# Trading the places of six groups in the first channel product of batch 0

## The chip, the cores and the metric

One Trainium2 chip, one core. The metric is the device time of one execution in microseconds. A comparison of this kernel tells about 2% from no change. The profile is of one execution, and its times are counted from the first instruction of the span.

## The reference

Two blocks follow each other. The first is attention over 4 batches, 8 heads, 768 positions and 64 columns a head; a position sees the first 4 positions and a window of 128. The second is an MLP over tokens and channels:

```
x   = attention(q, k, v)               # as 4 x 768 x 512
a1  = alpha1 * x + beta1
u   = x + lam * (w_tok @ a1)           # over the 768 positions
a2  = alpha2 * u + beta2
ch  = max(a2 @ w_ch1, 0) @ w_ch2       # 512 -> 2048 -> 512
out = u + lam * ch
```

The change touches `a2 @ w_ch1` of batch 0 alone.

## The kernel before

All inputs are float32 in HBM; products run in fp16 and gather in PSUM in float32. The program is a list of tasks, each of a few instructions on one engine. No scheduler runs while it is built: `emit` walks the tuple `ORDER` and issues the tasks by number. `ENGINES` gives the engine of each task that has a choice, and `HOMES` the buffer of each tile, so that a tile that needs a buffer waits for the last reader of the tile that had it before. Every engine carries out its tasks in the order in which they were issued.

The first channel product is made by `mlp1` (L921). It is cut into 16 groups of 128 columns of w_ch1 (`fi`, 0 to 15) and two halves of 384 positions (`chk`). A group is four matmuls of 128 x 384 (L929) into one PSUM tile `h`, one for each 128 rows of the depth of 512, followed by a relu that writes `hT`, on ACT (L935) or on DVE (L937). The operand `uT` is a2, transposed; for batch 0 it is made by PE transposes `uTp` (L890) of `u`, which ACT and DVE scale (L873, L875).

The weights w_ch1 are brought in by `load_w1` (L446) in four loads of 512 columns, so a quarter of the columns serves four groups: quarter 0 groups 0 to 3, quarter 1 groups 4 to 7, quarter 2 groups 8 to 11, quarter 3 groups 12 to 15. POOL issues them, one after another, with a conversion to fp16 on the way (L448), into `w1f`, which stays in SBUF for all batches. Each group waits for its quarter. `gate` (L453) puts tiny reads of quarters 1, 2 and 3 into the queue of SP (L455); SP waits at each until that quarter is there, and with it all loads that stand behind in its queue.

Around the place of the change these tasks stand on the engines, in this order. PE: token product `tok` (L849), transposes of the first half, the first groups of the half `chk` 0, then transposes of the second half, more groups, then the groups of `chk` 1, and between them transposes `tp` of batch 1's q and k (L507), its scores `S` (L617) and its products with the values, `pv` (L718). ACT: relus, casts of `u`, casts of q and k of batch 1 (L155). DVE: relus, the scaling of `uT`, and the product of staged w_ch2 with lam (L831, tile `w2f`). POOL: the other half of these products, and casts of the values of batch 1 (L157, tile `vfs`, from the load `vnat`). SP: loads of w_ch2 (L444, staged in four buffers `wst`), of batch 1's q and k (L397) and of its values (L407).

The second channel product of batch 0 (L1114) reads `hT` by quarters in their order and begins after all groups of the first.

Of the kernel before, what the change touches and what calls it, by code (L numbers as in the profile page):

```python
# [77 lines left out]
def kernel(  # L78
# [119 lines left out]
    for r in range(NR):  # L198
# [18 lines left out]
        26, 6, 9, 7, 10, 5, 11, 8, 18, 15, 72, 19, 1, 12, 3, 0, 4, 2, 22, 14, 73, 74, 45, 48, 46,  # L217
        17, 39, 49, 47, 53, 13, 40, 50, 41, 90, 95, 43, 91, 51, 54, 103, 52, 16, 44, 61, 104, 42,
        96, 109, 100, 62, 107, 110, 63, 55, 28, 108, 92, 56, 101, 21, 68, 65, 59, 93, 20, 69, 97,
        102, 111, 94, 24, 98, 57, 60, 30, 112, 105, 23, 58, 99, 113, 128, 106, 114, 116, 25, 131,  # L220
        135, 78, 115, 64, 27, 138, 31, 32, 117, 132, 29, 129, 136, 33, 122, 66, 125, 34, 123, 137,
        119, 139, 126, 35, 79, 70, 120, 140, 124, 84, 71, 80, 133, 130, 141, 67, 146, 85, 134, 121,
        147, 144, 75, 118, 158, 86, 154, 148, 159, 145, 142, 87, 149, 150, 155, 160, 143, 76, 88,
        151, 156, 81, 77, 166, 152, 162, 167, 89, 127, 82, 163, 213, 83, 168, 209, 164, 165, 214,
        210, 153, 217, 179, 211, 178, 157, 197, 229, 36, 212, 215, 218, 185, 216, 226, 230, 219,
        176, 161, 177, 220, 169, 223, 222, 232, 225, 224, 221, 227, 237, 233, 279, 238, 234, 228,
        273, 280, 182, 171, 204, 291, 274, 175, 289, 292, 200, 231, 293, 290, 246, 294, 295, 199,
        384, 241, 248, 188, 186, 257, 296, 247, 172, 243, 277, 174, 181, 242, 259, 258, 187, 170,
        278, 267, 37, 260, 271, 358, 268, 198, 285, 349, 272, 381, 301, 286, 366, 351, 303, 302,
        189, 297, 378, 173, 304, 281, 180, 352, 203, 249, 190, 282, 298, 379, 250, 287, 380, 192,  # L230
        353, 385, 288, 206, 283, 386, 369, 375, 367, 265, 284, 368, 202, 370, 266, 363, 376, 371,
        253, 377, 201, 299, 254, 372, 364, 183, 382, 191, 300, 373, 615, 365, 275, 374, 383, 357,
        261, 276, 408, 262, 387, 263, 184, 409, 205, 195, 239, 411, 264, 410, 395, 269, 396, 240,
        397, 270, 196, 388, 614, 621, 235, 412, 400, 194, 244, 398, 236, 401, 255, 617, 251, 245,
        256, 389, 390, 399, 252, 311, 359, 207, 193, 391, 424, 616, 335, 425, 393, 341, 426, 392,
        336, 648, 427, 634, 413, 394, 312, 636, 414, 428, 419, 404, 420, 415, 360, 405, 313, 429,
        208, 422, 337, 416, 361, 441, 421, 622, 402, 314, 423, 442, 626, 403, 305, 638, 315, 406,
        430, 640, 316, 435, 431, 306, 641, 355, 436, 443, 619, 437, 338, 649, 618, 438, 362, 317,
        432, 637, 407, 307, 433, 345, 444, 339, 439, 635, 318, 445, 450, 434, 639, 644, 319, 451,
        628, 452, 620, 440, 308, 645, 340, 453, 417, 446, 323, 447, 418, 320, 309, 448, 324, 321,  # L240
        658, 322, 329, 449, 642, 659, 454, 325, 625, 643, 330, 646, 347, 455, 326, 623, 343, 647,
        464, 344, 456, 465, 348, 466, 460, 457, 467, 650, 327, 458, 331, 461, 629, 459, 472, 462,
        632, 463, 653, 356, 651, 656, 627, 332, 38, 654, 480, 333, 342, 624, 652, 473, 310, 476,
        468, 471, 470, 469, 481, 474, 488, 885, 477, 475, 482, 492, 655, 490, 493, 350, 483, 478,
        514, 491, 516, 489, 657, 479, 515, 660, 517, 630, 882, 665, 518, 663, 354, 328, 666, 502,
        880, 661, 664, 498, 879, 519, 508, 499, 346, 503, 678, 662, 512, 509, 679, 504, 513, 487,
        484, 671, 485, 676, 486, 506, 677, 877, 548, 505, 672, 680, 507, 526, 549, 546, 527, 631,
        334, 522, 674, 681, 528, 547, 907, 523, 534, 903, 529, 633, 682, 675, 878, 542, 683, 535,
        890, 689, 543, 550, 685, 684, 690, 510, 551, 494, 511, 673, 667, 544, 495, 668, 891, 496,
        686, 545, 901, 687, 669, 497, 693, 888, 688, 883, 530, 694, 670, 700, 531, 524, 897, 701,  # L250
        698, 500, 691, 525, 696, 699, 552, 501, 697, 704, 553, 558, 695, 705, 904, 692, 562, 559,
        706, 909, 887, 707, 563, 564, 898, 708, 702, 566, 565, 910, 715, 703, 567, 532, 716, 889,
        713, 533, 709, 714, 896, 520, 710, 556, 717, 521, 538, 557, 537, 540, 539, 536, 560, 541,
        899, 718, 921, 572, 922, 881, 711, 574, 884, 573, 576, 712, 561, 719, 902, 577, 575, 555,
        727, 720, 569, 908, 721, 580, 728, 578, 722, 581, 729, 554, 723, 905, 730, 568, 739, 724,
        579, 725, 592, 570, 911, 726, 582, 740, 593, 588, 912, 583, 595, 584, 571, 906, 743, 589,
        731, 585, 900, 590, 732, 605, 744, 587, 733, 596, 606, 734, 607, 611, 594, 597, 602, 745,
        612, 586, 613, 599, 895, 603, 591, 757, 765, 600, 758, 601, 759, 766, 741, 771, 760, 742,
        916, 772, 751, 917, 746, 773, 752, 913, 761, 919, 774, 886, 767, 918, 604, 762, 763, 598,
        768, 777, 764, 779, 920, 923, 780, 914, 755, 915, 778, 608, 756, 926, 930, 735, 609, 931,  # L260
        924, 927, 781, 736, 925, 775, 782, 737, 928, 753, 929, 893, 738, 934, 754, 892, 769, 935,
        932, 610, 941, 770, 819, 776, 942, 894, 939, 820, 821, 940, 937, 936, 823, 749, 822, 945,
        748, 824, 938, 747, 827, 933, 948, 950, 750, 952, 943, 951, 825, 953, 787, 828, 944, 807,
        788, 797, 826, 808, 949, 946, 829, 798, 801, 954, 830, 791, 802, 956, 947, 792, 783, 955,
        957, 963, 961, 784, 789, 958, 962, 811, 790, 964, 959, 785, 812, 965, 805, 786, 795, 806,
        960, 967, 796, 799, 793, 968, 966, 970, 972, 794, 813, 971, 969, 815, 973, 814, 809, 800,
        816, 803, 810, 974, 978, 804, 976, 979, 837, 975, 977, 835, 838, 980, 841, 836, 839, 842,
        818, 843, 840, 845, 981, 832, 982, 846, 817, 986, 844, 831, 990, 987, 983, 988, 847, 991,
        984, 851, 833, 992, 1002, 993, 834, 848, 855, 852, 985, 849, 1003, 859, 856, 1004, 989,
        1006, 850, 860, 1005, 853, 998, 1007, 1008, 868, 999, 857, 1009, 997, 865, 995, 858, 862,  # L270
        996, 869, 866, 1000, 874, 994, 854, 1001, 1016, 863, 875, 1040, 1017, 1038, 1041, 1032,
        1039, 871, 1020, 872, 1028, 1021, 1011, 1024, 1029, 1013, 1018, 1033, 1012, 1025, 1034,
        1019, 1036, 1010, 1035, 1042, 1037, 1076, 1043, 1070, 1077, 870, 1074, 1071, 1054, 1075,
        1022, 1055, 1060, 1023, 1048, 1061, 1058, 1049, 1066, 1059, 1014, 1044, 1015, 1067, 1072,
        1045, 1056, 1073, 1026, 1057, 1078, 1068, 1079, 1064, 1069, 1046, 1027, 1050, 1063, 1047,
        1052, 1082, 1053, 1051, 1084, 1083, 1062, 1065, 1030, 1085, 1080, 1101, 1031, 1081, 1091,
        1102, 1107, 1092, 1097, 1093, 1103, 864, 1108, 1105, 867, 1098, 1111, 1106, 1104, 1113,
        1112, 1089, 1114, 1115, 1086, 1116, 1090, 861, 1094, 1087, 1117, 1099, 1109, 1100, 1121,
        1095, 1110, 1125, 1118, 1122, 1124, 1134, 1126, 1123, 1128, 1135, 1127, 1119, 1136, 1088,
        1140, 1120, 873, 876, 1131, 1129, 1141, 1096, 1137, 1142, 1132, 1130, 1133, 1138, 1139,  # L280
    )
    ENGINES = (
        "3313134433443333444444444444444433334441111201201202120212021213030121211201211210200200"
        "2020201202011202020202020213213213213213213202002020202020213121312131213121312131404444"
        "4044413314433334411114413334444042213221321021020121021021321202020020211212021212120212"
        "1212020202120202120212020212020202020212122221022221422221022221422221022221013111111131"
        "1311333333302002002102132002132002102020101212010321213120301212131201012121312010121213"
        "1203212131212131213421342104110121042104213401012020202021202020212120202020212120202121"
# [1034 lines left out]
```

The softmax here doesn't subtract the row's maximum and nothing guards it: scores larger than these inputs give would overflow.

## Time and profile before

| | us |
|---|---|
| runs shown, median (lowest to highest) | 258.79 (256.25 to 259.25), 3 runs |
| span of the profiled execution | 254.3 |
| whole time of the profiled execution | not given beside its span |
| PE busy with matmuls | 245.6 |
| DVE, ACT, POOL busy | 190.7, 133.2, 103.2 |
| mean granted TensorE clock | 0.997 |
| first channel product, matmuls of all batches | 89.8 |

The runs are whole device times; the span is counted from the first to the last instruction of the program, so the runs lie above it. Busy times of different engines lie beside each other. A row of the profile gives busy time, the mean duration of one instruction in ns, and then the idle time of that engine just before such instructions, with what ended it. Idle time counts for the kernel only where the engine is on the path that ends last.

### The profile page before, as it was taken

The numbers are of one execution on the slowest core, as the hardware profiler recorded it, in microseconds if no ns is written. First come the engines' busy times: TensorE is split into PE (matmuls) and PEld (weight loads), VectorE is DVE, ScalarE is ACT, GpSimd is POOL, SyncE is SP. The second block draws the span as 40 slices with busy tenths as digits, with TensorE's granted clock in tenths as the row PEclk, the third lists the DMA queues.
The fourth block names the chain that finished last, engine by engine and source line by source line (L and its number), as shares of the span: only waits on it lengthen the run. The fifth ranks groups of instructions, "written<-read, shape, count | busy, mean of one in ns | idle before, by whom it ended". The sixth has DMA issues, their size and how long they took to land.

```text
span 254.3 us, 5499 instructions
## 1 busy us (share of the span) xinstructions
PE 245.6 (97%) x2167; PEld 159.9 (63%) x2167; DVE 190.7 (75%) x402; ACT 133.2 (52%) x219; POOL 103.2 (41%) x124
## 2 busy tenths in 40 slices
PE   7799997999999999999999999999999999999993
PEld 7554644666555544566687686667667676667882
DVE  5688986767888874978879995578778983228892
ACT  2599913879977034787833434566660235543000
POOL 8318845876455527515782040065662120000010
PEclk9999999999999999999999999999999999999998
DMA  6999999899999999998484764520000140100327
GB/s 182 205 215 266 272 269 316 246 377 300 221 158 233 234 208 156 195 249 180 110 170 107 128 122 138 144 65 0 3 0 3 30 84 13 41 0 3 117 73 268
DMA packets 86129, 38.79 MB, mean 153 GB/s; under 512 B 73540, under 2 KB 80460, under 8 KB 86104
## 3 DMA queue, kind: packets, MB, share of 16 engines
q1 hardware_dynamic: 66576, 28.06, 47.3%
q10 hardware_dynamic: 15784, 7.11, 11.8%
q0 software_dynamic: 3744, 3.28, 8.0%
q8 instruction: 17, 0.28, 0.4%
q14 instruction: 8, 0.07, 0.1%
HBM read 29.91 MB, written 6.29 MB: 142 GB/s over the span
## 4 chain that ended last, share of the span: by engine, by line
PE 84%; DMA 11%; DVE 2%; POOL 1%; SPq 0%; issue 0%
PE h L929 32%; PE P L1046 22%; PE tok L849 9%; PE ch L1114 8%; DMA w1f<-in_moe_w_ch_dram 8%; PE pv L718 3%; PE S L617 3%; DMA nat<-in_k_dram 3%; PE tp L507 1%; POOL w1f L448 1%; PE tp L504 1%; DVE qkT L157 1%; DVE E L696 1%; PE pv L711 1%; PE pv L604 1%; PE idle L148 0%
## 5 line engine op out<-in xcount | busy, mean ns | idle before, releaser
L929 PE MATMUL h<-uT,w1f 128*128 128x384 f16 x512 | 89.8, 326 | 1.5 <-DMA w1f<-in_moe_w_ch_dram 1.5
L929 PEld LDWEIGHTS <-w1f 128*128 128x128 f16 x512 | 48.2, 98 | 32.7 <-DMA w1f<-in_moe_w_ch_dram 1.9
L935 ACT ACTIVATE hT<-h 128x384 f16<-128x384 f32 x77 | 37.0, 491 | 39.5 <-PE h L929 39.3
L937 DVE TENSOR_SCALAR hT<-h 128x384 f16<-128x384 f32 x51 | 27.8, 555 | 23.4 <-PE h L929 22.8
L1046 PEld LDWEIGHTS <-hT 128*128 128x128 f16 x408 | 39.5, 98 | 6.7 <-issue 0.2
L639 ACT ACTIVATE E<-S 128x1024 f16<-128x1024 f32 (+1 forms) x39 | 38.1, 1001 | 7.6 <-PE S L617 6.3
L762 POOL TENSOR_TENSOR tm<-x,la_b 128x512 f32<-128x512 f32 x18 | 24.3, 1353 | 24.2 <-DVE x L744 12.3
L849 PE MATMUL tok<-xh,wtokT 128*128 128x512 f16 x144 | 33.0, 379 | 0.0
L1059 DVE TENSOR_TENSOR x<-x,P 128x256 f32<-128x256 f32 x45 | 18.3, 419 | 11.3 <-PE P L1046 10.2
L1046 PE MATMUL P<-w2f,hT 128*128 128x256 f16 x216 | 26.5, 273 | 0.0
L849 PEld LDWEIGHTS <-wtokT 128*128 128x128 f16 x144 | 13.9, 98 | 15.0
L1114 PE MATMUL ch<-w2f,hT 128*128 128x512 f16 x96 | 23.2, 379 | 0.0
L1046 PE MATMUL P<-w2s,hT 128*128 128x256 f16 x192 | 23.1, 273 | 0.0
L1082 POOL TENSOR_TENSOR x<-x,pt 128x256 f32<-128x256 f32 x4 | 3.4, 854 | 47.5 <-DVE pt L1077 47.5
L155 ACT CAST u<-x 128x512 f16<-128x512 f32 x15 | 9.2, 615 | 24.9 <-DVE x L856 24.3
L744 DVE TENSOR_TENSOR x<-pv,rec 128x256 f32<-128x256 f32 x48 | 20.4, 425 | 1.7
L155 ACT CAST n<-nat 128x768 f16<-128x768 f32 x21 | 16.9, 828 | 8.9 <-DVE x L1125 6.4
L718 PEld LDWEIGHTS <-E 128*128 128x128 f16 x328 | 14.8, 98 | 5.1 <-issue 1.1
L856 DVE TENSOR_TENSOR x<-x,tok 128x512 f32<-128x512 f32 x24 | 16.0, 683 | 2.3 <-PE tok L849 2.3
L718 PE MATMUL pv<-vfs,E 128*128 128x65 f16 x328 | 17.7, 194 | 0.0
L579 POOL TENSOR_SCALAR_AFFINE_SELECT E<-E 128x512 f16<-128x512 f16 x12 | 7.5, 648 | 20.6 <-ACT E L639 20.6
L743 DVE RECIPROCAL rec<-pv 128x4 f32<-128x4 f32 x48 | 8.6, 179 | 7.2 <-PE pv L718 6.9
(134 smaller groups left out, 340.6 us busy)
## 6 DMA issues: line engine op xcount, KB each, us to landing
wst_w<-in_moe_w_ch_dram SPq DMA_DIRECT2D x8, 512.0 KB, 8.2
nat<-in_q_dram SPq DMA_DIRECT2D x10, 384.0 KB, 3.9
vnat<-in_v_dram SPq DMA_DIRECT2D x14, 256.0 KB, 5.7
nat<-in_k_dram SPq DMA_DIRECT2D x8, 384.0 KB, 7.2
out_dram<-x SPq DMA_DIRECT2D x11, 256.0 KB, 3.1
out_dram<-x ACTq DMA_DIRECT2D x10, 256.0 KB, 3.7
wtn<-in_moe_w_tok_dram SPq DMA_DIRECT2D x6, 384.0 KB, 4.1
w1f<-in_moe_w_ch_dram POOLq DMA_DIRECT2D x4, 512.0 KB, 15.4
```

The lines of the kernel that those rows point to most:

```text
L155: nc.scalar.copy(o, i)
L639: nc.scalar.activation(eT.t, pS.t[:, :, 0 : n * w].rearrange("p e (i w) -> p e i w", i=n), AF.Exp, scale=scale)
L718: nc.tensor.matmul(po.t[:, hl, :], eT.t[:, e_, off + i, c : c + P], vf[j][:, h, :], start=(r < 2 and n == 0), stop=(n == len(parts) - 1 an ...
L744: nc.vector.tensor_mul(bx.t[:, 4 * G : 4 * G + 4, :], po.t[:, :, 0:D], rec.t.to_broadcast([P, 4, D]))
L762: engine[e].tensor_mul(bt.t, bx.t.rearrange("p h d -> p (h d)"), la1_b)
L849: nc.tensor.matmul(pt.t, wtokT[:, si, ti * P : (ti + 1) * P], hs[si].t, start=(si == 0), stop=(si == NR - 1))
L929: nc.tensor.matmul(ph.t, w1f[:, c, fi * P : (fi + 1) * P], bu.t[:, c, chk * NTOK : (chk + 1) * NTOK], start=(c == 0), stop=(c == NC - 1))
L935: nc.scalar.activation(bh.t[:, fi, :], ph.t, AF.Relu)
L937: nc.vector.tensor_scalar_max(bh.t[:, fi, :], ph.t, 0.0)
L1046: nc.tensor.matmul(pc.t, hh[:, nt * P : (nt + 1) * P], w(fi), start=(first and n_ == 0), stop=(n_ == HF - 1), skip_group_check=True)
L1059: nc.vector.tensor_add(row(bx)[:, cols], row(bx)[:, cols], pc.t)
L1114: nc.tensor.matmul(pc.t, bh.t[:, fi, nt * P : (nt + 1) * P], w2f[:, fi, :], start=(fi == 0), stop=(fi == NF - 1))
```

## The change

Of the 16 groups of batch 0's first half, three of quarter 3 (13, 12, 14) and three others (4, 10, 5; quarters 1, 2 and 1) trade places in `ORDER`: their matmuls and their relus. The order of the first groups of this half on PE is, before and after (uTp are the transposes of the second half):

```
before:  1  11  8 | 13 12 14 | uTp | 15 | uTp |  4 10  5 | groups of the second half ...
after:   1  11  8 |  4 10  5 | uTp | 15 | uTp | 13 12 14 | groups of the second half ...
```

Tasks 257 and 258 are matmuls and relu of group 4, 259 and 260 of 5, 277 and 278 of 10, 289 and 290 of 12, 291 and 292 of 13, 293 and 294 of 14. The rest of the tuple keeps its order; in the file it is wrapped anew, so that lines after it stand 5 further down. `ENGINES` and `HOMES` change in four digits each: the relu at a place runs on the engine that it had there, and the PSUM tile at a place is the one that was there.

```diff
     ORDER = (
...
-        273, 280, 182, 171, 204, 291, 274, 175, 289, 292, 200, 231, 293, 290, 246, 294, 295, 199,
-        384, 241, 248, 188, 186, 257, 296, 247, 172, 243, 277, 174, 181, 242, 259, 258, 187, 170,
-        278, 267, 37, 260, 271, 358, 268, 198, 285, 349, 272, 381, 301, 286, 366, 351, 303, 302,
+        171, 204, 257, 274, 175, 277, 258, 200, 231, 259, 278, 246, 260, 295, 199, 384, 241,
+        248, 188, 186, 291, 296, 247, 172, 243, 289, 174, 181, 242, 293, 292, 187, 170, 290,
+        267, 37, 294, 271, 358, 268, 198, 285, 349, 272, 381, 301, 286, 366, 351, 303, 302,
...
     HOMES = (
...
-        "5011400001101201106367453322030011213032113023012132032032203212110303321023113113130113"
+        "5011400001101201106367453322030011213032113023012132032032203212113003321023113113103113"
```

## The prediction

> **What bounds the kernel now.** I read the page first: is there an engine that is full, and does it wait anywhere? TensorE (PE) has matmul work in 245.6 of the 254.3 us of the span, so any time that PE stands still near the change is time of the kernel, and time taken off any other engine is not.
>
> ```profile
> span 254.3 us, 5499 instructions
> PE 245.6 (97%) x2167; PEld 159.9 (63%) x2167; DVE 190.7 (75%) x402; ACT 133.2 (52%) x219; POOL 103.2 (41%) x124
> ...
> L929 PE MATMUL h<-uT,w1f 128*128 128x384 f16 x512 | 89.8, 326 | 1.5 <-DMA w1f<-in_moe_w_ch_dram 1.5
> ```
>
> The last line is the row of the first channel product (all batches): PE stands idle before it for 1.5 us in all, and what ends that idle time is a load of w1f. The chain that ended last, in order of time (start, length, what), shows where:
>
> ```profile
> 23.23 20.17 DMA w1f<-in_moe_w_ch_dram
> ...
> 43.45 2.12 PE h L929 x12
> 45.57 0.34 PE uTp L890 x6
> 45.91 0.65 PE h L929 x4
> 46.56 0.34 PE uTp L890 x6
> 46.89 7.15 PE h L929 x44
> ```
>
> From 43.45 us to the end the chain is PE work with no gap until the very last step on DVE. Before it stands one load, issued at 23.23 and landed 20.17 us later, at 43.40. The twelve matmuls that it releases are groups 13, 12 and 14. One group (4 matmuls) takes 0.65 us: the 44 matmuls of the last line are 11 groups in 7.15.
>
> Next, when are the other quarters of w1f there? The view of the tile w1f, and SP's own waits between 19 and 70 us (total, times, longest):
>
> ```profile
> L448 POOL DMA_DIRECT2D w1f<-in_moe_w_ch_dram x4: 750/766/814, 21.0 to 23.2; - x4
> ...
> DMA to landing us min/median/max: 9.6/15.4/20.2
> ```
> ```profile
> SPq L455 <- DMA w1f<-in_moe_w_ch_dram: 8.5, 1, 8.5
> SPq L444 <- DVE w2f L831: 4.3, 1, 4.3
> ```
> ```profile
> 35.96 0.80 SPq L455 DMA_DIRECT2D gates<-w1f  x1
> ...
> 46.19 0.37 SPq L444 DMA_DIRECT2D wst_w<-in_moe_w_ch_dram  x1
> ```
>
> The four loads are issued in the order of the quarters, at about 21.0, 21.8, 22.5 and 23.23 us. The first gate of SP waits for the second quarter (groups 4 to 7) and goes at 35.96: that quarter lands at 35.95, 14.2 us after its issue. The median of four is the mean of the middle two, so the third quarter takes 2 x 15.4 - 14.2 = 16.6 us and lands at about 39.1. The last one has the largest time, 20.2, and 43.40. PE reaches groups 13, 12, 14 at 41.95 (43.45 less the 1.50 us of idle time in its timeline). At that moment quarters two and three have been there for 6.0 and 2.8 us; the fourth alone is missing.
>
> Last, who stands behind this wait (timeline; in brackets the idle time before and its releaser):
>
> ```profile
> 44.31 0.49 ACT L935 ACTIVATE hT<-h 128x384 f16<-128x384 f32 x1 [2.57 <-PE h L929]
> 44.70 0.61 ACT L155 CAST u<-x 128x512 f16<-128x512 f32 x1
> ...
> 44.96 0.56 DVE L937 TENSOR_SCALAR hT<-h 128x384 f16<-128x384 f32 x1 [2.42 <-PE h L929]
> 45.43 0.68 DVE L831 TENSOR_TENSOR w2f<-wst_w,lam_b 128x512 f16<-128x512 f32 x1
> ```
>
> ACT waits 2.57 us and DVE 2.42 us for the delayed groups. Behind ACT's relu stands the cast of u (batch 0, row block 4) that the uTp transposes need; behind DVE's stands the w2f product that frees a staging buffer, for which SP waited 4.3 us (41.84 to 46.1) before its load at 46.19.
>
> [...] behind the one weight load that waits for the last quarter, PE does nothing for 1.50 us, though work with all its data stands a few instructions further on. [...] the granted clock stays 1.00 in every stretch of 1 us from 30 to 74, so I add nothing for a clock that the gap would have cost. [...]
>
> **The change, part by part.** No instruction is added or taken away. On PE the three groups right before the transposes of the second half (uTp) become 4, 10, 5 and the three right after them 13, 12, 14; group 15 stays between the two sets of transposes. In each place the PSUM buffer and the engine of the relu are those of before, so ACT, DVE, POOL and SP keep their order, and only the slice of w1f and hT differs. Relus of these groups are read only by the second product, from 68.2 us on; which of the six comes first does not matter there.
>
> Step 1, the wait removed. Group 4 can start at 41.95, as its quarter landed at 35.95; 10 needs the third (39.1, and PE had already run group 11 from it without a wait); 5 needs the second. Gain 1.50 us, all of it on PE.
>
> Step 2, what is late next. The fourth quarter is now first needed by group 15: 41.95 + 3 x 0.65 + 0.34 (transposes) = 44.24 us, or 44.41 with the 0.17 us that the first group after a gap shows in 2.12 against 1.95. It landed at 43.40, so 0.84 to 1.0 us are to spare and no wait returns. In a run where this load lands later, the change can hide at most 1.95 + 0.34 = 2.3 us.
>
> Step 3, the neighbours. Group 4's result reaches ACT 0.86 us after its start, as group 13's did (43.45 to 44.31): 42.81, relu to 43.30, cast of u to 43.8, and the transposes are due at 43.9, as close as before (45.31 against 45.41). The x blocks they need were done by 40.9 on DVE. ACT's next cast (45.99, now 44.5) needs a load that was issued at 36.87; the 7.1 us median of its kind puts it at 44.0. Nothing here costs more than 0.1 us.
>
> Step 4, the loads that follow. DVE's product moves from 45.43 to about 43.95, so the load at 46.19 goes at about 44.7 (POOL's half of the same buffer ends by 44.2), and the queue of SP behind it moves too. Is there room on the DMA engines? By stretches of 1 us (PE, PEld, DVE, ACT, POOL busy, clock, DMA share, GB/s):
>
> ```profile
> 47.00:48.00 1.00, 1.00 (x8) 0.59 (x6) 1.00 (x2) 1.00 (x3) 0.81 (x2) 1.00 0.85 104
> ...
> 49.00:50.00 1.00, 1.00 (x9) 0.61 (x7) 0.56 (x1) 0.84 (x2) 0.29 (x1) 1.00 0.84 161
> 50.00:51.00 1.00, 1.00 (x8) 0.61 (x7) 0.00 (x0) 0.68 (x3) 0.87 (x1) 1.00 0.69 224
> 51.00:52.00 1.00, 1.00 (x8) 0.61 (x7) 0.52 (x1) 1.00 (x3) 1.00 (x2) 1.00 1.05 395
> ```
>
> Against 395 GB/s, the first three leave (3 x 395 - 489) / 395 = 1.8 us of transfer unused; from 51 us on the engines are full. A queue that starts 1.5 us earlier fits into this hole, and the full stretch behind it moves with it.
>
> Step 5, the tightest meeting with a load later on is the value block of batch 1:
>
> ```profile
> 67.82 0.93 POOL L157 CAST vfs<-vnat 128x512 f16<-128x512 f32 x1 [0.70 <-DMA vnat<-in_v_dram]
> ...
> 69.19 0.41 PE L718 MATMUL pv<-vfs,E 128*128 128x65 f16 x8
> ```
>
> POOL waits for the load, casts until 68.75, and PE uses the result at 69.19 to 69.22: 0.45 us to spare. If the loads did not move, PE would stop here and only 0.45 us of the gain would be left; if they move by at least 1.05 us nothing is lost. By step 4 they do. I take off 0.1 us for moves that are not complete.
>
> Sum: 254.3 - 1.5 + 0.1 = 252.9 us for the profiled span. Of the profiled execution only the span is given; the runs shown lie 2.0 to 5.0 us above it (256.25 to 259.25), the median 4.5. Around the work I change nothing: 258.79 - 1.4 = 257.4 us. The gain is 0.5%, and about 2% is what a measurement of this kernel can tell from no change.
>
> **Rivals.** First, the gain is taken back at the value block: the DMA engines are full from 51 us to beyond 70, which speaks for it; the hole before 51 speaks against. It gives 258.79 - 0.45 = 258.3. Second, the wait in usual runs is longer than in the profiled one, as a landing after 20 us in a crowd of loads can vary: the limit of step 2 gives 258.79 - 2.3 = 256.5. For it: all runs shown are longer than the span by at least 2 us; against: nothing says that they lose it here. Third, slower: ACT's own load of batch 2 (issued at 64.25, 384 KB) follows the faster PE and starts 1.5 us earlier, while SP's queue does not move; [...] the value block lands later. At the 218 GB/s that the same answer shows from 66 to 73 us, sharing 1.5 us costs the value load at most 1.5 us; the kernel is slower than before once the load is over 0.45 us later than now, and at worst by 1.5 - 0.45 = 1.05 us, in the middle by 0.5: 259.3. Against it: SP's queue is released by the same PE work.
>
> **How the numbers follow.** My forecast 0.56 (257.4, own range 256.9 to 257.7), taken back 0.22 (258.3), longer wait 0.10 (256.5), slower 0.10 (259.3), anything else 0.02. These cases span 256.5 to 259.8; the runs of one kernel spread over 3 us, so a median can lie some 1.5 us lower with the luck of its runs, less upwards, as two of the three shown lie at the top. Range 254.9 to 259.5. None of the cases reaches 2% (5.2 us): faster by over that 0.03, within 0.95, slower 0.02, the rest being what neither view shows.
>
> **What would show it.** Right: PE's idle time before the row of h falls from 1.5 us to under 0.2; the load of w1f is gone from the chain that ended last, which then runs back through PE work before 42 us; SP's load of 46.19 stands near 44.7; POOL's value cast near 66.4 and PE's use of it near 67.7, with no idle time; the span near 252.9. Wrong: a wait of PE for w1f at group 15, or at an earlier group on its second or third quarter; PE idle before the pv row near 68 us (taken back); the value cast at or after 68.3 (slower).

## The result, and the profile after

The changed kernel takes 255.7 us (median of 16 runs, 254.13 to 262.14) beside 258.28 us for the kernel before on the same chip (16 runs). The ratio is 0.9938, with a 95% interval of 0.9908 to 0.9967: 0.62%, or 1.6 us, faster. In a second comparison it gave 0.9948 [0.9919, 0.9977]. Both lie far inside the 2% named ahead; that there is a gain rests on two intervals that both stay under 1. The forecast was a gain of 1.4 us. All ratios here leave out runs over 1.5% above the fastest of their kernel, so the medians, which hold every run, lie further apart (2.6 us here, 2.3 us in the second comparison), and from the five single profiles below that are of such runs (before_c, e2_q3_earlier, e3_15_later, e7_loads_first, e9_late_and_loads) I read what happens, not the gain.

The profiled execution of the changed kernel took 255.43 us, 2.2 us more than its span. First the page of the kernel after: span, busy times of the engines, and the row of the first channel product (busy time, mean ns, idle time before it):

```profile
span 253.2 us, 5499 instructions
PE 245.4 (97%) x2167; PEld 159.8 (63%) x2167; DVE 190.7 (75%) x402; ACT 133.3 (53%) x219; POOL 102.2 (40%) x124
...
L934 PE MATMUL h<-uT,w1f 128*128 128x384 f16 x512 | 89.6, 327 | 0.0
```

The work of every engine is that of before, to within 1 us. What is gone is the 1.5 us of idle time at the end of the last row, and with it the releaser, the load of w1f. The chain that ended last of the kernel after (start, length, what) passes the place without a load:

```profile
40.56 3.90 PE h L934 x24
44.46 0.34 PE uTp L895 x6
44.80 0.65 PE h L934 x4
45.45 0.34 PE uTp L895 x6
45.78 7.15 PE h L934 x44
```

The 24 matmuls are groups 1, 11, 8, 4, 10, 5 in one piece; 24 x 0.1625 = 3.90, so nothing stands between them. The two spans differ by 1.1 us, less than the wait, because the first of these groups began 0.57 us later than in the profile before (40.40 against 39.83 on the timeline). That has nothing to do with the change: the transposes of w_tok already begin at 24.11 instead of 23.54, and near 10 us PE had waited 0.99 us for a cast of DVE where it waited 0.26 before. The sum is -1.50 (the wait) -0.17 (the slow first group after the gap) +0.57 = -1.10; the first transposes stand at 44.46 instead of 45.57, and the end at 253.2 instead of 254.3. From the transposes on, nothing more is won or lost.

The load itself did not come earlier. The tile w1f of the kernel after, and the timeline of PE at the group that is now the first to need the last quarter:

```profile
L453 POOL DMA_DIRECT2D w1f<-in_moe_w_ch_dram x4: 747/765/812, 21.3 to 23.6; - x4
...
DMA to landing us min/median/max: 8.6/14.0/20.9
```
```profile
40.40 4.06 PE L934 MATMUL h<-uT,w1f 128*128 128x384 f16 x24
...
44.63 0.81 PE L934 MATMUL h<-uT,w1f 128*128 128x384 f16 x4
```

The last of the four is issued at 23.59 and lands 20.9 us later, at 44.50, which is 1.1 us later than in the profile before. Group 15 starts at 44.63. In this execution the order of before would have waited some 2.0 us (an estimate: 44.50 less 40.56 + 1.95, when PE is done with three groups), more than the 1.5 us that it was seen to wait; the new order covers it with 0.13 us to spare.

Then what stands behind: the timeline of the kernel after on DVE, on SP, on POOL and on PE, the same instructions that the prediction followed.

```profile
43.85 0.56 DVE L942 TENSOR_SCALAR hT<-h 128x384 f16<-128x384 f32 x1 [0.74 <-PE h L934]
44.33 0.91 DVE L836 TENSOR_TENSOR w2f<-wst_w,lam_b 128x512 f16<-128x512 f32 x1
```
```profile
45.31 0.37 SPq L449 DMA_DIRECT2D wst_w<-in_moe_w_ch_dram  x1
```
```profile
65.96 0.61 POOL L157 CAST vfs<-vnat 128x512 f16<-128x512 f32 x1
```
```profile
68.08 0.41 PE L723 MATMUL pv<-vfs,E 128*128 128x65 f16 x8
```

DVE's relu waits 0.74 us where it waited 2.42. Its w2f product goes at 44.33 (45.43 before), SP's load at 45.31 (46.19), and the cast of the values finds its data there: the 0.70 us that POOL waited for `vnat` are gone, and the cast ends at 66.57, 1.5 us before PE uses it (0.45 before). The hole in the transfers is filled, as the view by stretches of 1 us shows for the kernel after (the last number is GB/s):

```profile
47.00:48.00 1.00, 1.00 (x8) 0.61 (x7) 0.39 (x1) 0.84 (x3) 1.00 (x2) 1.00 0.77 271
...
49.00:50.00 1.00, 1.00 (x8) 0.59 (x6) 0.84 (x1) 0.77 (x2) 0.57 (x1) 1.00 0.97 347
50.00:51.00 1.00, 1.00 (x9) 0.60 (x7) 0.56 (x1) 1.00 (x3) 0.61 (x1) 1.00 1.05 386
```

Before, these three stretches moved 104, 161 and 224 GB/s.

### The profile page after: what moved, and what is told of

Its sections match the earlier page's. It is cut to its first block, busy times and chain, and to the rows that moved or that the text cites. A ratio compares the mean times of both kernels' runs of the same rounds, so it can differ in the third digit from the quotient of the medians.

```text
span 253.2 us, 5499 instructions
## 1 busy us (share of the span) xinstructions
PE 245.4 (97%) x2167; PEld 159.8 (63%) x2167; DVE 190.7 (75%) x402; ACT 133.3 (53%) x219; POOL 102.2 (40%) x124
## 4 chain that ended last, share of the span: by engine, by line
PE 94%; DMA 3%; DVE 0%; SPq 0%; issue 0%
PE h L934 33%; PE P L1051 22%; PE tok L854 12%; PE ch L1119 8%; PE pv L723 5%; PE S L622 4%; DMA nat<-in_k_dram 3%; PE S L617 2%; PE tp L512 1%; PE pv L716 1%; PE tp L509 1%; PE wT L814 1%; PE sk L554 1%; PE idle L148 1%; PE uTp L895 1%; PE pv L609 1%
```

## The experiments

My theory: PE's wait for the last quarter is the cost, and what the change does is to let other groups go in its place. Rivals: the gain comes from the loads of SP's queue, which the same step starts earlier, and not from PE's wait; or it comes from something else in the new places (buffers, relus, another spread of PE's work).

| kernel | against before | median us (runs) |
|---|---|---|
| the change | 0.9938 [0.9908, 0.9967] | 255.7 (16) |
| the change, again | 0.9948 [0.9919, 0.9977] | 255.37 (14) |
| e1_mirror | 0.992 [0.9891, 0.9949] | 255.08 (14) |
| e5_one_group | 0.9964 [0.9935, 0.9992] | 257.03 (22) |
| e2_q3_earlier | 1.0057 [1.0025, 1.0088] | 259.31 (22) |
| e7_loads_first | 0.9957 [0.9926, 0.9989] | 257.1 (22) |
| e4_loads_held | 0.9986 [0.9955, 1.0018] | 257.27 (22) |
| e3_15_later | 0.9905 [0.987, 0.994] | 255.01 (11) |
| e6_q3_late | 0.9893 [0.9862, 0.9923] | 255.23 (13) |
| e10_after_loads | 0.9921 [0.9889, 0.9953] | 254.84 (15) |
| e9_late_and_loads | 0.9891 [0.9838, 0.9944] | 254.64 (6) |

**The mirror: keep the order of the groups, turn the order of the loads.** `ORDER` is that of before; quarter 3 is loaded second and quarter 1 last, and the gates follow.

```diff
+    TURN = {1: 3, 3: 1}
     def load_w1(p, i):
+        i = TURN.get(i, i)
     def gate(i):
+        i = TURN.get(i, i)
```

> The kernel before, with its order of groups kept. The loads of quarters 1 and 3 of w1f trade places in POOL's queue, and the gates of SP follow them, so that SP waits for the same load numbers. If the gain came from the wait for the last load alone, this mirror must give it too: PE idle before the row of the first product falls from 1.5 us to under 0.2 us, ratio to before 0.994 (0.991 to 0.997). If the gain came from something else about the new order of groups (which slice of hT or w1f is touched when), the wait goes but the time stays: ratio 0.998 to 1.002.

Measured: 0.992 [0.9891, 0.9949], the gain of the change. The row of its page:

```profile
L933 PE MATMUL h<-uT,w1f 128*128 128x384 f16 x512 | 89.6, 326 | 0.0
```

No group, buffer or relu has moved here, so the third theory falls: what counts is that the groups at this place read a quarter that has landed. Between PE's wait and the loads that hang on it the mirror does not decide, as both move.

**One group of the three.** Before, with only 13 and 4 traded (tasks 291, 292 and 257, 258). The order becomes 1 11 8 4 12 14.

```diff
-        171, 204, 291, 274, 175, 289, 292, 200, 231, 293, 290, 246, 294, 295, 199, 384, ...
-        188, 186, 257, 296, 247, 172, 243, 277, 174, 181, 242, 259, 258, 187, ...
+        171, 204, 257, 274, 175, 289, 258, 200, 231, 293, 290, 246, 294, 295, 199, 384, ...
+        188, 186, 291, 296, 247, 172, 243, 277, 174, 181, 242, 259, 292, 187, ...
```

> The kernel before with only groups 13 and 4 trading places, so quarter 3 is needed one group, 0.65 us, later. Wait theory: idle time falls by 0.65 us, to about 0.85 us with the landing of the profile, ratio 0.9975, some 40% of the whole change. If only the first group of a set matters, the whole gain: 0.994.

Measured: 0.9964 [0.9935, 0.9992]. The interval reaches from almost no gain to all of it, but on this chip the mirror's median is 255.08 us and this one's 257.03, so one group does not bring what the whole change brings. PE's timeline:

```profile
43.04 1.47 PE L929 MATMUL h<-uT,w1f 128*128 128x384 f16 x8 [0.35 <-DMA w1f<-in_moe_w_ch_dram]
```

One group of cover (0.65 us) leaves a wait of 0.35 us for a load that landed at 42.99 this time. The dose goes the right way.

**The other way: the last quarter sooner.** Before, with 13 traded for 11 and 12 for 8, so that the order is 1 13 12 11 8 14 and the last quarter is needed 1.3 us earlier.

```diff
-        ..., 233, 279, ..., 273, 280, 182, 171, 204, 291, 274, 175, 289, 292, ...
+        ..., 233, 291, ..., 289, 292, 182, 171, 204, 279, 290, 175, 273, 280, ...
```

> The kernel before, with groups 13 and 12 ahead of 11 and 8 (these trade places), so quarter 3 is needed two groups, 1.30 us, earlier. The wait theory says that PE's idle time is landing less arrival, so it grows by 1.3 us, to 2.8 us in a run with the profile's landing, and the kernel gets slower by 1.3 us less nothing: ratio 1.005. A theory by which waits at this place are caught up later (the loads behind bound the stage) says that idle time grows and the span does not: ratio 1.000.

Measured: 1.0057 [1.0025, 1.0088], slower by 1.5 us, where the groups came 1.3 us earlier. In the profiled run PE waits 4.24 us for a landing at 44.57, and something follows that the profile before had not shown. PE's timeline, and the view by stretches (PE, PEld, DVE, ACT, POOL busy, clock, DMA share, GB/s):

```profile
44.62 4.66 PE L929 MATMUL h<-uT,w1f 128*128 128x384 f16 x14 [4.24 <-DMA w1f<-in_moe_w_ch_dram]
```
```profile
43.00:44.00 1.00, 0.00 (x0) 0.00 (x0) 0.00 (x0) 0.00 (x0) 0.83 (x1) 0.77 1.20 308
44.00:45.00 1.00, 0.38 (x2) 0.22 (x3) 0.00 (x0) 0.00 (x0) 0.03 (x1) 0.50 1.09 334
...
48.00:49.00 1.00, 1.00 (x4) 0.45 (x3) 0.00 (x0) 0.33 (x1) 1.00 (x2) 0.50 0.04 14
```

Fourteen matmuls take 4.66 us instead of 2.3: the granted clock falls to 0.50 while PE waits and stays there until 50.4. At the same time the DMA engines run empty (14 GB/s), since SP's next load waits for DVE (8.4 us), DVE for its relu, and that for PE. So this wait of PE costs a second time, through the clock: half of 44.62 to 50.4, that is 2.9 us. That the late loads cost PE much a third time does not show: the span is 7.5 us longer than that of before_b below, whose first group began at the same 39.56 and which has no wait, and the wait and the clock make up 7.1 of them.

**The kernel before, twice more.** Was 1.5 us the usual wait? The same kernel, one profiled execution each.

> The kernel before once more, for a second look at what an execution loses after the wait. Theory (two parts: the wait itself, and loads that start late because of it): PE's idle time before the first product is about 2 us, as the last quarter landed later than 43.4 in most profiles taken so far, and in an execution near the median PE also stops between 54 and 69 us for batch 1's casts or values, 0.3 to 1.5 us in all. Rival (the wait is all): no stop of PE after 46 us.

> As before_b, a third look at the kernel before: idle time of PE before the first product about 2 us, and stops between 54 and 69 us in an execution near the median.

Measured: 254.15 us and 259.63 us, for one program. The spans and the row of the first channel product, of before_b and then of before_c:

```profile
span 252.4 us, 5499 instructions
...
L929 PE MATMUL h<-uT,w1f 128*128 128x384 f16 x512 | 89.6, 326 | 0.0
```
```profile
span 257.9 us, 5499 instructions
...
L929 PE MATMUL h<-uT,w1f 128*128 128x384 f16 x512 | 91.2, 330 | 2.8 <-DMA w1f<-in_moe_w_ch_dram 2.8
```

In before_b the last load landed at 41.24 and PE did not wait at all: this run of the old order is as quick as those of the new one. In before_c it landed at 45.23. The chain of before_c at that place, to be held against the same lines of before in the prediction:

```profile
23.04 22.19 DMA w1f<-in_moe_w_ch_dram
45.23 0.05 issue
45.28 3.06 PE h L929 x12
48.34 0.64 PE uTp L890 x6
48.98 1.08 PE h L929 x4
50.06 0.33 PE uTp L890 x6
50.39 7.15 PE h L929 x44
```

From the end of the wait to the 44 matmuls it is 5.11 us here and 3.44 us in the profile before (43.45 to 46.89), for the same instructions. The 1.67 us are the clock: by stretches of before_c it is 1.00 up to 46, then

```profile
46.00:47.00 1.00, 1.00 (x6) 0.54 (x5) 0.00 (x0) 0.86 (x2) 1.00 (x2) 0.66 0.67 235
47.00:48.00 1.00, 1.00 (x5) 0.46 (x4) 0.91 (x2) 0.14 (x1) 1.00 (x1) 0.50 0.20 53
48.00:49.00 1.00, 1.00 (x9) 0.79 (x7) 0.60 (x1) 0.63 (x2) 0.38 (x2) 0.50 0.17 55
49.00:50.00 1.00, 1.00 (x6) 0.51 (x5) 0.98 (x3) 0.58 (x1) 1.00 (x2) 0.64 0.00 2
```

and 1.00 again while PE works. The deficits are 0.34 + 0.50 + 0.50 + 0.36 = 1.70 us, which is 3.4 us at half clock. So the 5.5 us between these two spans are 0.8 us of an earlier scatter (first group at 40.38 against 39.56), 2.8 us of wait, 1.7 us of clock, and 0.2 us that I do not place.

Both expectations also said that PE stops for late loads between 54 and 69 us, and that missed. From 38 us to the end no wait of PE is listed for before_b, and for before_c this one alone (total, times, longest):

```profile
PE h L929 <- DMA w1f<-in_moe_w_ch_dram: 2.8, 1, 2.8
```

So no profile of the kernel before shows a time that PE loses to the loads behind the wait.

How often is that so? Each run comes with its mean granted clock, and the 3.4 us at half clock of before_c take 1.7 / 255 = 0.0067 from it. Of 135 runs of the kernel before, beside the experiments, 44 have a clock under 0.9945, and of 89 runs of kernels that read the last quarter later or load it sooner (the change twice, e1, e3, e6, e9, e10) 6. Between them lie e5 with 2 of 22, e4 with 3 of 22 and e7 with 6 of 22; e2, which needs the quarter sooner, has 14 of 22. The count roughly follows the wait, but a mean does not tell where the clock fell: in the profiles of e3 and e9, two of the six, it fell near 31 us, ahead of the place. The ratio of 0.9938 does not hang on such runs: those above 0.9945 alone have medians of 257.0 us (before, in each of the two larger sets) and 255.4 us (the change, both times). Over all runs the change saves more, 2.3 to 2.6 us by the medians.

**The changed kernel again, beside these.**

> The changed kernel itself, beside the other three on the same chip. Ratio to before 0.991 to 0.997, as measured, PE idle before the row of the first product 0.0 to 0.5 us.

Measured: 0.9948 [0.9919, 0.9977]; span 252.6 us, no idle time before the row. SP's load went at 44.69, POOL's value cast at 65.34 and PE's use of it at 67.46, beside 44.7, 66.4 and 67.7 in the prediction: here the first group began at 39.78, as in the profile before (39.83).

**Is it the wait, or the loads behind it?** Two kernels try to move one and not the other. In the first, the order before is kept, and DVE makes its w2f product (task 199) ahead of a relu that hangs on PE's wait, so that SP's load is free earlier while PE waits as before:

```diff
-        ..., 293, 290, 246, 294, 295, 199, 384, ...
+        ..., 293, 199, 290, 246, 294, 295, 384, ...
```

> The kernel before, but DVE makes the second half of the w2f product of block 12 ahead of the relu of group 12, which waits for PE; so the SP load at 46.19 us goes at about 44.2, as early as in the changed kernel or earlier, while PE keeps its wait for the last quarter of w1f. Wait theory: PE's wait stays at about 1.5 us and the ratio is 1.000 (0.998 to 1.002). Rival (the gain of the change is that SP's loads start earlier): ratio 0.994 to 0.996 without the wait gone.

Measured: 0.9957 [0.9926, 0.9989]. The theory of the wait alone expected no gain, and by this ratio it missed, narrowly: the interval lies just under 1. The medians say less: 257.1 us beside 257.68 for the kernel before on this chip, and 255.37 for the change. Its timelines of PE, SP and ACT:

```profile
44.30 3.58 PE L929 MATMUL h<-uT,w1f 128*128 128x384 f16 x12 [2.11 <-DMA w1f<-in_moe_w_ch_dram]
```
```profile
44.82 0.37 SPq L444 DMA_DIRECT2D wst_w<-in_moe_w_ch_dram  x1
49.15 1.46 SPq L397 DMA_DIRECT2D nat<-in_q_dram  x3
```
```profile
47.91 0.49 ACT L935 ACTIVATE hT<-h 128x384 f16<-128x384 f32 x1 [1.56 <-PE h L929]
48.30 0.82 ACT L155 CAST n<-nat 128x768 f16<-128x768 f32 x1
```

The wait is there, with the drop of the clock behind it (0.50 from 45 to 48 us, 12 matmuls in 3.58 us). SP's load goes 1.4 us sooner than in the profile before, but the next loads in its queue stand until 49.15: they wait for a buffer that ACT's cast at 48.30 frees, and that cast stands behind a relu that waits for PE. So only one load moved, and what it brings by itself lies between nothing and a part of the gain.

In the second, the order is the new one, but DVE's product and SP's loads behind it (tasks 186, 172, 174) stand behind the relu of group 13:

```diff
-        295, 199, 384, 241, 248, 188, 186, 291, 296, 247, 172, 243, 289, 174, 181, 242, 293, 292, 187,
+        295, 384, 241, 248, 188, 291, 296, 247, 243, 289, 181, 242, 293, 292, 199, 186, 172, 174, 187,
```

> The changed kernel, but DVE makes the second half of the w2f product of block 12 three instructions later (after the scaling of uT, the product of block 0 and the relu of group 13), so the staging buffer comes free later and the SP load that stood at 45.31 us in its profile goes at about 48.0; the queue behind it moves too. Nothing else is changed. If the gain needs the loads to move with PE (step 4 and 5), the value cast of batch 1 (65.96 us) lands 2 to 2.7 us later, PE must wait for batch 1's casts and values between 54 and 69 us for 0.5 to 1.5 us, and the ratio to the kernel before is 0.996 to 0.999. If the loads have room anyway, there is no wait and the ratio stays at 0.993.

Measured: 0.9986 [0.9955, 1.0018]: PE has no idle time before the first product, and the gain is nearly gone. Its timelines of SP, POOL and PE:

```profile
47.37 0.37 SPq L449 DMA_DIRECT2D wst_w<-in_moe_w_ch_dram  x1
```
```profile
67.43 0.61 POOL L157 CAST vfs<-vnat 128x512 f16<-128x512 f32 x1 [1.88 <-DMA vnat<-in_v_dram]
```
```profile
68.09 0.37 PE L723 MATMUL pv<-vfs,E 128*128 128x65 f16 x7 [0.27 <-POOL vfs L157]
```

The load goes at 47.37, later even than before (46.19), though PE is not late. POOL waits 1.88 us for the values, casts until 68.04, and PE stops for 0.27 us at just the meeting that the prediction called the tightest (and for 0.3 us before transposes `tp`, for a cast of POOL). This profile is of the quickest run of this kernel (254.93 us), and the stop is small in it; that its other runs (median 257.27) lose over 2 us at the same place is a guess, and not shown. What is shown is that a freed PE keeps little of the gain if these loads fall back: 257.27 us beside 255.37 for the change on the same chip. As they fell back further than in the kernel before, the run does not tell what is left if they merely stay.

**More cover.** If 0.13 us of spare at group 15 is little, does more of it help? In e3_15_later, the changed kernel with 15 traded for 9; in e6_q3_late moreover 13 for 6 and 12 for 7, so that no group reads the last quarter before the third place behind the transposes:

```diff
-        260, 295, 199, ..., 186, 291, 296, ..., 289, ..., 293, 292, ...
+        260, 275, 199, ..., 186, 261, 276, ..., 263, ..., 293, 262, ...
```

> The changed kernel, and groups 15 and 9 trade places too, so quarter 3 is first needed after the second set of transposes, 1.0 us later than in the changed kernel. In the profile of the changed kernel group 15 started 0.13 us after the last load had landed, so in about half of the runs it must wait a little. Wait theory: no idle time at all, ratio to the kernel before 0.992 to 0.994, that is 0.1 to 0.5 us better than the changed kernel. If landings scatter less than that: equal to the changed kernel, 0.994.

> The changed kernel, and groups 15 and 9, 13 and 6, 12 and 7 trade places, so of quarter 3 only group 14 stands early, as third after the second set of transposes, 2.3 us later than group 15 in the changed kernel. If last-quarter landings later than that of the profile still cost the changed kernel something, this is better than the changed kernel by 0.2 to 0.7 us (ratio to before 0.990 to 0.992, PE idle 0.0). If the changed kernel's wait is gone in nearly all runs, equal to it: 0.993.

Measured: 0.9905 [0.987, 0.994] and 0.9893 [0.9862, 0.9923], both with no idle time before the row. That is a little lower than was expected (0.992 to 0.994 and 0.990 to 0.992), but no gain over the change is shown. In the profile of e6 PE waits for no load of w1f; it comes to the first group of the last quarter at about 47.8 (an estimate: 46.54, when the second set of transposes is done, and two groups of 0.65), and the latest landing read from a profile here is 45.23 (before_c). Beside e6 on the same chip the changed kernel had 0.9948 [0.9919, 0.9977], the two intervals just overlap, and the medians are 255.23 and 255.37 us. (In e3's profile PE stood idle for 4.77 us up to 32.19, until a product of DVE, so nothing is read from its place.)

**The loads sooner as well.** The changed kernel, and e6, with DVE's product ahead of the relu before it:

```diff
-        ..., 259, 278, 246, 260, 295, 199, 384, ...
+        ..., 259, 199, 278, 246, 260, 295, 384, ...
```

> The changed kernel, and DVE makes the second half of the w2f product of block 12 ahead of the relu of group 10, so the staging buffer no longer waits for PE but for POOL's half alone, and SP's load goes about 0.6 us earlier than in the changed kernel. If late loads still cost the changed kernel anything, ratio to before 0.990 to 0.993; if not, equal to it: 0.994.

> The changed kernel with both: quarter 3 of w1f needed late (groups 15 and 9, 13 and 6, 12 and 7 traded) and the w2f product of block 12 ahead of the relu of group 10. No idle time of PE before the first product, ratio to before 0.988 to 0.992, and not slower than either part alone. If the two parts touch the same time: 0.990 to 0.993.

Measured: 0.9921 [0.9889, 0.9953] and 0.9891 [0.9838, 0.9944]. They are the lowest medians of the study (254.84 and 254.64 us), but neither interval is clear of that of the change. In e10's profile the spare at group 15 was not enough:

```profile
44.39 0.82 PE L934 MATMUL h<-uT,w1f 128*128 128x384 f16 x4 [0.28 <-DMA w1f<-in_moe_w_ch_dram]
```

The load landed at 44.35 and PE had come 0.28 us too soon. I take e6's order as the safer one; that it beats the change is not established.

## Why the prediction was right

**Step 1, the wait removed.** Right in place and cause: the row has no idle time, the chain no load, and the mirror gives the same gain without moving a group. But the 1.50 us was one draw from a wide spread. In the three profiles of the order before the wait was 0.0, 1.5 and 2.8 us, and the last load of w1f landed between 41.24 and 45.23 us in nine profiles (before, before_b, before_c, the change, e2, e5, e7, e9, e10), in the middle at 44.35. PE came to the place at 41.95 in the profile before, so the usual wait is, by estimate, about 2.4 us: the rival of a longer wait was right in part.

**Step 2, what is late next.** The prediction had 0.84 to 1.0 us to spare at group 15, "and no wait returns". That is the step that was too sure: it took a landing of 43.40 as fixed. The change's own profile had 0.13 us to spare, and e10, with the same groups in the same places, waited 0.28 us. The limit of 2.3 us of cover was sized rightly, and the landings reach beyond it (45.23 in before_c, where 41.95 + 2.3 is 44.25).

**Step 3, the neighbours.** Right. ACT's relu of group 4 begins at 43.20, that is the predicted 42.81 plus most of the 0.57 us by which PE came later, and the transposes follow at 44.46 with no gap.

**Step 4, the loads.** Right. DVE's product was put at 43.95 and came at 44.33, SP's load at 44.7 and came at 45.31 (44.69 in the second run of the change); the hole before 51 us took the transfers. The prediction saw the moved loads as a condition for keeping the gain. e4 agrees: with the loads held back almost nothing is left. e7 shows that one load sooner does not stand in for the wait, as its median stays 1.7 us above that of the change.

**Step 5, the value block.** The place was right, as the stop of 0.27 us in e4 shows. The 0.1 us taken off for incomplete moves was not lost; the spare grew from 0.45 to 1.5 us. The rival "taken back" did not come, nor did the slower one: SP's queue moved with PE.

**The clock.** The prediction added nothing for it, as the profile before showed 1.00 in every stretch around the place. For that execution it was right. It was wrong as a rule for all of them: the wait of before_c cost 1.7 us more this way, and a third of the runs of before have a mean clock that is lower by as much or more.

**The sum.** Span 252.9 forecast, 253.2 measured (252.6 the second time). The prediction put 4.5 us around the span, from a median of three runs against one span. In every comparison the median of that difference was 1.7 to 2.2 us. The 2.5 us too many were no time around the work: the profiled execution was one of the quicker runs, with a wait shorter than usual. As the forecast was taken from the median and not from the span, the slip did no harm to the difference: 1.4 us less was foretold and 1.6 us found. The 257.4 us itself is 1.7 us above the measured 255.7. That lies inside the whole range (254.9 to 259.5), but below the forecast's own (256.9 to 257.7), and nearer to the rival of a longer wait (256.5). Some 0.5 us of it is the median of before, 258.79 in three runs and 258.28 in the sixteen beside the change. The rest lies in terms sized from one execution, the wait of step 1 and the clock: by the medians of all runs the change saves 2.6 us, not 1.4. So the place, the cause and the direction were reasoned out; that 1.4 and 1.6 agree so closely is luck in part.

**Open.** How the 1.6 us split between the wait and the loads stays open: SP's queue hangs on PE, so neither e4 nor e7 moves one of the two alone, and the profiles of the kernel before show the wait and the clock, but no stop of PE for the loads. Why the last load lands anywhere in 4 us (41.24 to 45.23) is open too: the runs show that it does, not why.

## What to carry to other kernels

The load that PE waited for here landed anywhere between 41.24 and 45.23 us in nine profiles; look at such a landing in several executions, and put work behind it that covers its late end and not only the wait of one profile. Before trading places, follow the queue of loads that hangs on the stalled engine through buffers and neighbours: in e4, where they fell back, the freed engine kept almost none of the gain. Do not count a wait of the matrix engine at its length alone: behind those of 2.1, 2.8 and 4.2 us here stood another 1.7 to 2.9 us of lost clock (2.9 in e2: half of 44.62 to 50.4); behind the 1.5 us of before stood none.

## What the runs showed of the hardware

The granted clock of TensorE fell to 0.50 behind gaps of PE of 2.11 us (e7) and 2.79 us (before_c), and within the one of 4.24 us (e2). Behind gaps of 1.50 us (before), 0.35 us (e5) and 0.28 us (e10) it stayed at 1.00. In before_c the fall came 1.0 us after PE had begun again (at about 46.3, by the 0.66 of the stretch from 46 to 47, where PE began at 45.28). What the stretches lack of 1.00 adds up to 1.70 us in before_c, 1.71 in e7 and 3.42 in e2, which is 3.4, 3.4 and 6.8 us at 0.50. The length of the longest gap does not sort these runs by itself: in e9 the clock fell near 31.5 us (its mean from 20 to 42 us is 0.92), behind gaps of only 1.37 and 0.37 us (timeline of PE, and by stretches):

```profile
30.17 0.42 PE L723 MATMUL pv<-vfs,E 128*128 128x65 f16 x8 [1.37 <-DVE x L749]
30.43 0.50 PE L814 MATMUL wT<-iden,wt 128*128 128x128 f16 x6
31.29 0.63 PE L814 MATMUL wT<-iden,wt 128*128 128x128 f16 x6 [0.37 <-ACT wt L819]
```
```profile
31.00:32.00 1.00, 0.71 (x9) 0.71 (x10) 0.97 (x4) 1.00 (x3) 0.95 (x2) 0.77 1.14 291
32.00:33.00 1.00, 0.94 (x11) 0.47 (x9) 0.33 (x1) 0.96 (x3) 1.00 (x3) 0.50 1.12 284
```

What makes the clock fall after one gap and not after another, these runs do not show.

The four loads of w1f, issued one after another by one engine, scatter by microseconds among the other loads: in before_b, before and before_c the quickest took 7.0, 9.6 and 11.0 us and the last one 18.5, 20.2 and 22.2 us, for the same 512 columns each, in one and the same program.
